# Scratch rows of a two-step Fourier transform laid every other row, so that its DMAs move 48 and 56 rows of one stride

## The chip, the cores and the metric

The kernel runs on one core of one Trainium2 chip. The metric is the device time of one execution in microseconds (us); lower is better. TensorE (PE) multiplies matrices, VectorE (DVE), ScalarE (ACT) and GpSimd (POOL) work on tiles, and SyncE (SP) does nothing here but issue DMAs, one after the other.

## The reference

```python
# x: (8, 3136, 256); w_r, w_i: (256, 256)
X = rfft(x, axis=1)
Yr = Xr @ w_r - Xi @ w_i + b_r
Yi = Xr @ w_i + Xi @ w_r + b_i
Y = soft_threshold(Yr, 0.01) + 1j * soft_threshold(Yi, 0.01)
a = irfft(Y, n=3136, axis=1)
u = a + real(fft(fft(a, axis=1), axis=2))
un = (u - mean(u)) / sqrt(var(u) + 1e-6)          # over the last axis
out = u + relu(un @ w_ch1) @ w_ch2                # 256 -> 1024 -> 256
```

## The kernel before

The sequence of 3136 = 64 x 49 is transformed in two steps, and back in two steps, with a pass through DRAM after each first step, since rows have to change places between partitions and the free axis. There are eight batches `b`. For each of them:

- `p1` multiplies by the 64-point table and folds the inputs `n2` and `49 - n2` into their sum and difference (`fold`). Of the 49 inputs, 24 pairs and one single (number 24 of `NM` = 25) remain. The results go to a DRAM scratch `ad` (for the first batch to four pieces `aq`).
- `p2_f2` (the helper `rows_f2`, line 532) loads the rows that one group of four frequencies `u` needs into a tile `af`: half `i` = 0 at partition 0 and half `i` = 1 at partition 64, one DMA for each half. A half holds 25 rows of sums and 25 rows of differences. Tables `tff` are loaded beside it. Matmuls of line 570 multiply them.
- `p2_w` multiplies by the weights and thresholds; `p2_mix` makes the second Fourier transform's part (scratch `md`, tiles `mq`); `p2_yt` transposes.
- `p2_g2` (line 794) does the first step back: its result is copied by ACT (line 813) into a tile `bev` and stored with two DMAs of line 816 for each `bev` into the DRAM scratch `bd`. A half again is 25 rows of sums and 25 of differences.
- `p3_norm` loads `bd` (tiles `bf`, line 871) and `md` (tiles `mt`, lines 885 to 890), takes the second step back and the norm; `p3_tr`, `p3_mlp1` and `p3_mlp2` transpose and run the two dense layers with their matmuls `h` and `o` (helper `mm3`, line 179). At the end of a group of up to 512 columns, line 982 multiplies `o` by the row scale into a tile `t` on DVE.

Two points matter for what follows. First, `t` shares its two buffers with the copies `bev`:

```python
bev = sb.tile([128, 512], F32, tag="bf" if odd else "bev", bufs=4 if odd else 2, name="bev")   # line 812
t = rb if k else sb.tile([128, 512], F32, tag="bev", bufs=2, name="t")                         # line 981
```

so line 982 can run only when the stores that read an earlier `bev` have landed. Second, every DMA is on SP's one queue, in the order in which the program was laid out, and each takes one of eight semaphores in turn (`DMAHW0` to `DMAHW7`): a DMA is issued only when the one eight places ahead of it has landed.

The order of the work of different batches is written out by due times (each `yield` of a task is one), and a scheduler then orders the instructions. Scratch tensors `ad` and `bd` have the shape `[2, NM, 2, U, D]`: sum or difference, which of 25, half, frequency (32), column (256).

Of the kernel before, what the change touches and what calls it, by code (L numbers as in the profile page):

```python
# [62 lines left out]
def tables():  # L63
    n1 = np.arange(N1)
    n2 = np.arange(N2)

    fwd = np.zeros((2, N1, 2, 2, U))
    inv = np.zeros((2, 2, U, 2, 2, 32))
    n1h = rows_n1()
    for s in range(2):  # L70
        for u in range(U):
            ph = 2 * np.pi * ((n1 * u) % N1) / N1
            if u == 0:
                alt = np.where(n1 % 2, -1.0, 1.0)
                fwd[s, :, s, 0, 0] = 1.0
                fwd[s, :, s, 1, 0] = alt
                inv[s, 0, 0, s] = 1.0
                inv[s, 1, 0, s] = np.where(n1h % 2, -1.0, 1.0)
            else:
                fwd[s, :, s, 0, u] = np.cos(ph)  # L80
                fwd[s, :, s, 1, u] = -np.sin(ph)
                phh = 2 * np.pi * ((n1h * u) % N1) / N1
                inv[s, 0, u, s] = 2 * np.cos(phh)
                inv[s, 1, u, s] = -2 * np.sin(phh)
    tf = np.zeros((2, 64, U, S))
    ti = np.zeros((2, 64, U, 64))
    kp = np.append(np.arange(1, NM), 0)
    P, M = slice(0, NM), slice(NM, 2 * NM)
    for u in range(U):
        t, sg = slot_freqs(u)  # L90
        m = len(t)
        ph = 2 * np.pi * (np.outer(kp, t) % N) / N
        co, si = np.cos(ph), np.sin(ph)
        if u == 0:
            w = np.full(50, 2.0)
            w[[0, 49]] = 1.0
            for c in range(2):
                j = slice(25 * c, 25 * c + 25)
                tf[c, P, 0, j] = co[:, j]
                tf[1 - c, M, 0, j] = -si[:, j]  # L100
                ti[c, j, 0, P] = (co * w)[:, j].T / N
                ti[1 - c, j, 0, M] = (-si * w)[:, j].T / N
        else:
            tf[0, P, u, :m] = co
            tf[0, M, u, :m] = si
            tf[1, P, u, :m] = co * sg
            tf[1, M, u, :m] = -si * sg
            ti[0, :m, u, P] = co.T / N
            ti[0, :m, u, M] = si.T / N
            ti[1, :m, u, P] = (co * sg).T / N  # L110
            ti[1, :m, u, M] = -(si * sg).T / N
    p = np.arange(128)
    ph = 2 * np.pi * (np.outer(p, np.arange(129)) % D) / D
    cs = np.stack([np.cos(ph), np.sin(ph)], 1)
    cs[0, 1, 0] = 1.0
    mask = np.ones((128, 2))
    mask[0] = 0.0
    mask[:, 1] *= -1.0
    first = fwd.reshape(128, 2, 2, 4, 8).transpose(0, 3, 1, 2, 4).reshape(128, 128)
    out = dict(  # L120
        fwd=fwd.reshape(128, 128), fwd0=first, inv=inv.reshape(128, 128),
        tf=tf.reshape(128, U, S), ti=ti.reshape(128, U, 64),
        cs=cs, mask=mask, ident=np.eye(128),
    )
    return {k: np.ascontiguousarray(v, dtype=np.float32) for k, v in out.items()}
# [11 lines left out]
T = 10000  # L137
E = 32
MR = NH + 64 + E

SHAPE0, STEP0 = (0.25, 0.25, 0.6), 0.15
SHAPE, STEP1, STEP = (0.395, 0.569, 0.36), 0.2, 0.25
# [8 lines left out]
def spectral_block(ctx: ExitStack, tc: tile.TileContext, x, w_ri, b_ri, w1, w2,  # L151
# [171 lines left out]

    def pair_rows(t, kp):

        rows = t.shape[2] * t.shape[3] * D
        return bass.AP(t.tensor, t.offset + kp * rows, [[D, 2 * rows // D], [NM * rows, 2], [1, D]])

    def tile_rows(t, i, u, n):

        half = t.shape[3] * D
        return bass.AP(t.tensor, t.offset + i * half + u * D, [[2 * (NM - i) * half + half, 2], [2 * half, NM], [1, n * D]])

    def fold(g, out, copied):

# [11 lines left out]
    def p1_first():  # L347


        aq = [dr.tile([2, NM, 2, 8, D], F32, tag=f"aq{q}", bufs=1, name=f"aq{q}") for q in range(4)]  # L350
        ad1 = dr.tile([2, NM, 2, U, D], F32, tag="ad", bufs=4, name="ad1")
        a_dram[0] = lambda u: (aq[u // 8], u % 8)
        a_dram[1] = lambda u: (ad1, u)

# [11 lines left out]

        def store(q, ev, mb, nn, single):
            if single:
                src = ev[32 * q:32 * q + 16, :D].unsqueeze(1).to_broadcast((16, 2, D))
                return st_eng.dma_start(out=aq[q][:, mb].rearrange("s c u d -> (c u) s d"), in_=src)  # L370
            rows = 16 * D
            src = ev[32 * q:32 * q + 32, :nn * D].rearrange("p (n s d) -> p n s d", s=2, d=D)
            for i in range(2):
                dst = bass.AP(aq[q].tensor, aq[q].offset + (i * NM + mb) * rows, [[D, 32], [2 * rows, nn // 2], [1, D]])
                d = st_eng.dma_start(out=dst, in_=src[:, :, i])
            return d

# [40 lines left out]
        ev, mb = rest[0][:2]  # L418
        for q, c in np.ndindex(4, 2):
            with tc.issue_after(af_ld[3]):  # L420
                st_eng.dma_start(out=ad1[:, mb, c, 8 * q:8 * q + 8].rearrange("s u d -> u s d"),
                                     in_=ev[32 * q + 16 + 8 * c:32 * q + 24 + 8 * c, :D].unsqueeze(1).to_broadcast((8, 2, D)))

    def ask(b, ci, todo, slots, pre):

# [41 lines left out]
    def p1(b):  # L467
# [3 lines left out]
            return  # L471
        for i in (b, b + 1)[:1 + (b % 2 == 0)]:
            if i not in a_dram:
                ad = dr.tile([2, NM, 2, U, D], F32, tag="ad", bufs=4, name=f"ad{i}")
                a_dram[i] = lambda u, ad=ad: (ad, u)
        todo = [(m, 4) for m in range(0, NM - 1, 4)] + [(NM - 1, 1)] * (b % 2 == 0)
        t0, width = T1 if b == 1 else (b - 0.3, 0.75) if b > 2 else (2.0, 0.48)
# [8 lines left out]
        while ci < len(todo):  # L486
            yield T * (t0 + width * ci / len(todo))
            if todo[ci][1] == 1:
                ask(b, ci, todo, slots, pre)
                m, xf = todo[ci][0], pre[ci]  # L490
                g = gtile("g_f1")
                te.matmul(g[:, :D], fwd_f, xf[:, :D], start=True, stop=True)
                ev = xf[:, D:2 * D]
                sc.copy(ev, g[:, :D])
                for r in range(2):
                    st_eng.dma_start(out=a_dram[b + r](0)[0][:, m].rearrange("s c u d -> (c u) s d"),
                                     in_=ev[r * 64:r * 64 + 64].unsqueeze(1).to_broadcast((64, 2, D)))
                ci += 1
                continue
            groups = []  # L500
            for c in range(ci, ci + (1 if b == 1 else 2)):
                ask(b, c, todo, slots, pre)
                i = slots[c][3]
                xf = pre[c - i][:, i * 1024:i * 1024 + 1024]
                groups.append(([gtile("g_f1") for _ in range(2)],
                               [[xf[64 * r:64 * r + 64, p * 512:p * 512 + 512] for p in range(2)] for r in range(2)], xf[0:1, 0:2]))
            quarters(fwd_f, groups)
            for c, (banks, movs, late) in enumerate(groups, ci):
                i, m = slots[c][3], todo[c][0]
                xf = pre[c - i][:, i * 1024:i * 1024 + 1024]  # L510
                for r, g in enumerate(banks):
                    ev = xf[:, r * 512:r * 512 + 512]
                    fold(g, ev, ev[:, D:])
                    st_eng.dma_start(out=pair_rows(a_dram[b](0)[0], m + 2 * r), in_=ev.rearrange("p (s d) -> p s d", d=D))
            ci += len(groups)
# [16 lines left out]
    def rows_f2(b, q, s):  # L532

        u0 = 8 * q
        tag = "tot" if b == 0 and (2 * q + s) % 3 == 2 else "af"
        af = sb.tile([128, 4 * D], F32, tag=tag, bufs=2, name="af")
        ad, u = a_dram[b](u0 + 4 * s)
        load = nc.sync.dma_start
        for i in range(2):
            ld = load(out=af[64 * i:64 * i + 50], in_=tile_rows(ad, i, u, 4))  # L540
        tff = sb.tile([128, 4, S], F32, tag="tff", bufs=3, name="tff")
        load(out=tff, in_=c_tf[:, u0 + 4 * s:u0 + 4 * s + 4, :])
        if b == 0:
            af_ld[2 * q + s] = ld.ins
            done.add(("af", 2 * q + s))
        return af, tff

    def p2_f2(b):


        for q in range(4):
# [12 lines left out]
            for s in range(2):  # L564
                yield base + STEP * F2W * s / 2

                def one(i, t, k, j):
                    rows = slice(64 * i, 64 * i + 50)
                    first = t * D + k * 128 + j * 64
                    return te.matmul(banks[i][64 * j:64 * j + 64, k * 200 + t * S:k * 200 + t * S + S], afs[s][rows, first:first + 64],  # L570
                                     tfs[s][rows, t], start=True, stop=True)
# [221 lines left out]

    def p2_g2(b):

        bd = b_dram[b] = dr.tile([2, NM, 2, U, D], F32, tag="bd", bufs=4, name=f"bd{b}")
        for q in range(4):
            base, STEP, F2W, W0, WW, M0 = clock2(b, q)
            for s in range(2):
# [10 lines left out]
                for i, g in enumerate(banks):  # L810
# [2 lines left out]
                    sc.copy(bev, g)  # L813
                    for h in range(2):
                        j = i ^ h
                        st_eng.dma_start(out=tile_rows(bd, i, 8 * q + 4 * s + 2 * h, 2), in_=bev[64 * j:64 * j + 50])  # L816
        done.add(("b", b))


# [7 lines left out]
    def p3_norm(b):  # L827
# [36 lines left out]
        def load(m, n):  # L864
            mt = sb.tile([128, 4, D], F32, tag="mt", bufs=2, name="mt")
            bfs = [sb.tile([128, 512], F32, tag="bf", bufs=4, name="bf") for _ in range(1 + (n > 1))]
            for r in range(2):
                if n == 1:
                    nc.sync.dma_start(out=bfs[0][64 * r:64 * r + 64, :D], in_=b_dram[b - 1 + r][0, m].rearrange("c u d -> (c u) d"))
                else:  # L870
                    nc.sync.dma_start(out=bfs[r].rearrange("p (s d) -> p s d", d=D), in_=pair_rows(b_dram[b], m + 2 * r))
            for r in (1, 0):
# [213 lines left out]
```

## Time and profile before

| | |
|---|---|
| median of 3 runs | 2291.35 us (2291.03 to 2292.4) |
| profiled execution | 2296.82 us, span of its instructions 2294.9 us |
| PE busy | 1854.8 us, 81% of the span |
| DVE, ACT, POOL busy | 1185.5, 785.8, 537.2 us |
| mean granted clock of TensorE | 0.89 |
| DMA packets' time, of 16 engines | 34.0% of the span on SP's queue |

The profiled execution is 5.5 us above the median, and 1.9 us of it lie outside its span. PE is the busiest engine. The profile's chain of work that ended last follows the execution back from its end, at each step to what released it; a DMA in it is counted from issue to landing.

### The profile page before, as it was taken

The numbers are of one execution on the slowest core, as the hardware profiler recorded it, in microseconds if no ns is written. First come the engines' busy times: TensorE is split into PE (matmuls) and PEld (weight loads), VectorE is DVE, ScalarE is ACT, GpSimd is POOL, SyncE is SP. The second block draws the span as 40 slices with busy tenths as digits, with TensorE's granted clock in tenths as the row PEclk, the third lists the DMA queues.
The fourth block names the chain that finished last, engine by engine and source line by source line (L and its number), as shares of the span: only waits on it lengthen the run. The fifth ranks groups of instructions, "written<-read, shape, count | busy, mean of one in ns | idle before, by whom it ended". The sixth has DMA issues, their size and how long they took to land.

```text
span 2294.9 us, 36930 instructions
## 1 busy us (share of the span) xinstructions
PE 1854.8 (81%) x13447; PEld 1457.6 (64%) x13447; DVE 1185.5 (52%) x2754; ACT 785.8 (34%) x1957; POOL 537.2 (23%) x1005
## 2 busy tenths in 40 slices
PE   6674295887969858988787958989696979898999
PEld 4343174666758647766566747767475758676888
DVE  3553264555646545555454634655463736565554
ACT  1343242333434423433332423323243434342222
POOL 0000132222323212232221412313232323222210
PEclk8776597988989979999898978999898998999999
DMA  5443334334432433324432343322433224224211
GB/s 167 156 132 99 95 117 128 100 99 137 138 108 70 140 116 110 96 68 135 132 117 75 102 141 98 116 83 88 139 125 97 80 86 118 92 59 125 78 33 41
DMA packets 166902, 242.97 MB, mean 106 GB/s; under 512 B 25025, under 2 KB 110657, under 8 KB 166465
## 3 DMA queue, kind: packets, MB, share of 16 engines
q1 hardware_dynamic: 166720, 240.62, 34.0%
q8 instruction: 106, 1.74, 0.3%
q14 instruction: 76, 0.61, 0.1%
HBM read 136.19 MB, written 104.36 MB: 105 GB/s over the span
## 4 chain that ended last, share of the span: by engine, by line
PE 55%; DMA 25%; DVE 8%; SPq 6%; issue 3%; ACT 2%; POOL 1%; DVEq 0%; POOLq 0%; ACTq 0%
PE o L179 21%; PE h L179 17%; DMA bd<-bev 11%; DMA af<-ad 5%; PE g_w L179 5%; DMA af<-aq 2%; PE g_g L808 2%; PE g_f L570 2%; DMA out_dram<-total 2%; PE g_yt L789 2%; SPq L816 1%; SPq L889 1%; PE g_f L439 1%; PE g_ut L932 1%; DVE ut L835 1%
## 5 line engine op out<-in xcount | busy, mean ns | idle before, releaser
L179 PE MATMUL o<-hl,w2h 128*128 128x512 f32 (+2 forms) x832 | 351.5, 423 | 234.8 <-DVE t L982 222.8
L951 DVE SCALAR_TENSOR_TENSOR hl<-h,hh 128x512 fp32r<-128x512 f32 (+2 forms) x416 | 271.6, 655 | 358.2 <-ACT hh L950 344.7
L950 ACT ACTIVATE hh<-h 128x512 fp32r<-128x512 f32 (+2 forms) x416 | 237.6, 572 | 636.7 <-PE h L179 467.2
L179 PEld LDWEIGHTS o<-hl,w2h 128*128 128x128 f32 x832 | 168.7, 203 | 304.7 <-DVE t L982 230.2
L179 PE MATMUL o<-hh,w2l 128*128 128x512 f32 (+2 forms) x832 | 333.7, 401 | 0.0
L179 PE MATMUL o<-hh,w2h 128*128 128x512 f32 (+2 forms) x832 | 333.7, 401 | 0.0
L179 PE MATMUL h<-utl,w1h 128*128 128x512 f32 (+2 forms) x832 | 325.2, 391 | 6.3 <-DVE hl L951 6.3
L179 PE MATMUL h<-uth,w1l 128*128 128x512 f32 (+2 forms) x832 | 320.0, 385 | 0.0
L179 PE MATMUL h<-uth,w1h 128*128 128x512 f32 (+2 forms) x832 | 319.5, 384 | 0.0
L958 POOL TENSOR_TENSOR total<-uth,utl 128x256 f32<-128x256 f32 x200 | 145.0, 749 | 462.9 <-DMA out_dram<-total 306.5
L982 DVE TENSOR_TENSOR t<-o,rb 128x512 f32<-128x512 f32 (+2 forms) x52 | 34.2, 658 | 298.8 <-DMA bd<-bev 259.4
L179 PEld LDWEIGHTS o<-hh,w2l 128*128 128x128 f32 x832 | 168.6, 203 | 31.3
L179 PEld LDWEIGHTS h<-utl,w1h 128*128 128x128 f32 x832 | 160.6, 193 | 40.9 <-DVE hl L951 9.1
L179 PEld LDWEIGHTS o<-hh,w2h 128*128 128x128 f32 x832 | 169.8, 204 | 23.2 <-issue 0.8
L179 PEld LDWEIGHTS h<-uth,w1l 128*128 128x128 f32 x832 | 159.6, 192 | 30.1 <-issue 2.4
L179 PEld LDWEIGHTS h<-uth,w1h 128*128 128x128 f32 x832 | 160.1, 192 | 26.6 <-issue 0.4
L647 DVE SCALAR_TENSOR_TENSOR y<-g_w,small,ks 128x400 f32<-128x400 f32 x128 | 80.2, 627 | 109.9 <-ACT ks L642 55.1
L570 PE MATMUL g_f<-tff,af 50*64 50x50 f32 x4096 | 85.2, 240 | 43.2 <-ACT g_f L458 22.4
L570 PEld LDWEIGHTS g_f<-tff,af 50*64 50x64 f32 x4096 | 76.6, 153 | 65.3 <-ACT g_f L458 25.3
L650 POOL TENSOR_TENSOR Y<-y,m 128x400 f32<-128x400 f32 x56 | 61.6, 1100 | 219.0 <-DVE m L649 206.1
L789 PE MATMUL g_yt<-ident,Y 128*128 128x128 f32 x496 | 89.0, 300 | 27.2 <-POOL Y L650 15.1
L813 ACT COPY bev<-g_g 128x512 f32<-128x512 f32 x128 | 69.2, 588 | 87.7 <-PE g_g L808 56.8
(170 smaller groups left out, 3102.4 us busy)
## 6 DMA issues: line engine op xcount, KB each, us to landing
bd<-bev SPq DMA_DIRECT2D x256, 100.0 KB
bf<-bd SPq DMA_DIRECT2D x96, 256.0 KB
out_dram<-total SPq DMA_DIRECT2D x88, 256.0 KB
af<-ad SPq DMA_DIRECT2D x112, 200.0 KB
ad<-xf SPq DMA_DIRECT2D x84, 256.0 KB
md<-mq SPq DMA_DIRECT2D x112, 192.0 KB
xf<-in_x SPq DMA_DIRECT2D x39, 512.0 KB
mt<-md SPq DMA_DIRECT2D x192, 64.0 KB
```

Of the source, the lines that this page charges most:

```text
L179: last = te.matmul(o, l, r, start=start and i == 0, stop=stop and i == 2)
L439: return te.matmul(banks[i][64 * j:64 * j + 64], mat[rows, rows], movs[i][j], start=True, stop=True)
L570: return te.matmul(banks[i][64 * j:64 * j + 64, k * 200 + t * S:k * 200 + t * S + S], afs[s][rows, first:first + 64], tfs[s][rows, t], sta ...
L647: va.scalar_tensor_tensor(y1, gw, bias[:, c, o:o + 1], ks, op0=ALU.add, op1=ALU.add)
L650: (va if b == 0 or o == 0 else gp).tensor_sub(y[:, o, :, c, :], y1, m)
L789: te.transpose(gt[:, (v * 2 + o) * 128:(v * 2 + o + 1) * 128], z.rearrange("p c w -> p (c w)"), ident)
L808: return te.matmul(banks[i][64 * j:64 * j + 64, cols], tif[rows, 2 * h + v], ys[h][rows, cols], start=True, stop=True)
L813: sc.copy(bev, g)
L950: sc.activation(hh[:, :w], h[:, :w], AF.Relu)
L951: va.scalar_tensor_tensor(hl[:, :w], h[:, :w], 0.0, hh[:, :w].bitcast(F32), op0=ALU.max, op1=ALU.subtract)
L958: gp.tensor_add(total[:, k, cols], uth[:, k, cols].bitcast(F32), utl[:, k, cols].bitcast(F32))
L982: va.tensor_mul(t[:, :w], o, rb[:, :w])
```

## The change

The scratch tensors become `[2 * 56, U, D]`. Even rows belong to half 0 and odd rows to half 1. Of half `i`, rows `i`, `i + 2`, ... hold 24 rows of sums, the single row (row 48 for half 0, row 97 for half 1), and 24 rows of differences. The single is stored once, not as sum and as difference. `tile_rows` now is one run of rows of one stride. `rows_f2` issues three DMAs, not two: 48 rows for each half, and one of two rows (96 and 97, the last of each half) into partitions 48 and 112. `p2_g2` stores 56 rows for each half, of which the last seven lie behind the 49 that are read. The single rows are stored and loaded by two DMAs where there was one. The tables are reordered to match, and the matmuls of line 570 contract over 49 rows, not 50.

```diff
@@ tables: rows of the two halves
-    kp = np.append(np.arange(1, NM), 0)
-    P, M = slice(0, NM), slice(NM, 2 * NM)
+    kp = np.arange(NM)
+    P = [np.append(r, np.arange(NM - 1)) for r in (NM - 1, 2 * NM - 2)]
+    M = [np.arange(NM, 2 * NM - 1), np.arange(NM - 1, 2 * NM - 2)]
@@ constants
+RT = 56
@@ helpers
     def pair_rows(t, kp):
-        rows = t.shape[2] * t.shape[3] * D
-        return bass.AP(t.tensor, t.offset + kp * rows, [[D, 2 * rows // D], [NM * rows, 2], [1, D]])
+        rows = t.shape[1] * D
+        return bass.AP(t.tensor, t.offset + 2 * kp * rows, [[D, 4 * rows // D], [(2 * NM - 1) * rows, 2], [1, D]])
-    def tile_rows(t, i, u, n):
-        half = t.shape[3] * D
-        return bass.AP(t.tensor, t.offset + i * half + u * D, [[2 * (NM - i) * half + half, 2], [2 * half, NM], [1, n * D]])
+    def tile_rows(t, i, u, n, r=RT):
+        rows = t.shape[1] * D
+        return bass.AP(t.tensor, t.offset + i * rows + u * D, [[2 * rows, r], [1, n * D]])
+    def zero_rows(t, c, u=0, n=None):
+        return t[(2 * NM - 2) + (2 * NM - 1) * c, u:u + (n or t.shape[1])]
@@ p1_first, store of the single row (p1 alike)
-                src = ev[32 * q:32 * q + 16, :D].unsqueeze(1).to_broadcast((16, 2, D))
-                return st_eng.dma_start(out=aq[q][:, mb].rearrange("s c u d -> (c u) s d"), in_=src)
+                for c in range(2):
+                    d = st_eng.dma_start(out=zero_rows(aq[q], c), in_=ev[32 * q + 8 * c:32 * q + 8 * c + 8, :D])
+                return d
@@ rows_f2
         for i in range(2):
-            ld = load(out=af[64 * i:64 * i + 50], in_=tile_rows(ad, i, u, 4))
+            load(out=af[64 * i:64 * i + N2 - 1], in_=tile_rows(ad, i, u, 4, N2 - 1))
+        ld = load(out=af[N2 - 1::64], in_=ad[2 * N2 - 2:2 * N2, u:u + 4].rearrange("r u d -> r (u d)"))
@@ p2_f2, one
-                    rows = slice(64 * i, 64 * i + 50)
+                    rows = slice(64 * i, 64 * i + N2)
@@ p2_g2
-        bd = b_dram[b] = dr.tile([2, NM, 2, U, D], F32, tag="bd", bufs=4, name=f"bd{b}")
+        bd = b_dram[b] = dr.tile([2 * RT, U, D], F32, tag="bd", bufs=4, name=f"bd{b}")
-                        st_eng.dma_start(out=tile_rows(bd, i, 8 * q + 4 * s + 2 * h, 2), in_=bev[64 * j:64 * j + 50])
+                        st_eng.dma_start(out=tile_rows(bd, i, 8 * q + 4 * s + 2 * h, 2), in_=bev[64 * j:64 * j + RT])
@@ p3_norm, load of the single row
-                    nc.sync.dma_start(out=bfs[0][64 * r:64 * r + 64, :D], in_=b_dram[b - 1 + r][0, m].rearrange("c u d -> (c u) d"))
+                    for c in range(2):
+                        nc.sync.dma_start(out=bfs[0][64 * r + 32 * c:64 * r + 32 * c + 32, :D], in_=zero_rows(b_dram[b - 1 + r], c))
```

The order of the matmuls on PE and of the work of DVE, ACT and POOL stays the same but for a few neighbours that change places. On SP's queue the program has 1740 DMAs, not 1658. Three places of that queue, with the semaphores that each DMA waits for (the names are tiles and scratch tensors as above, with the numbers of their buffers, and the size is that of the DMA's destination; `PE`, `Activation` and `DVE` are waits for those engines):

The first `af` loads of the program, before:

```order
L316 DMA small_100<-in_b_ri 128x4
L540 DMA af_279<-aq0_114 50x1x1024 x2
L540 DMA af_284<-aq0_114 50x1x1024 x2
L316 DMA ident_98<-c_ident 128x128
L316 DMA csf_330<-c_cs 128x258
```

and after:

```order
L315 DMA small_100<-in_b_ri 128x4
L543 DMA af_280<-aq0_114 48x1024 x2
L544 DMA af_280<-aq0_114 2x1024
L543 DMA af_286<-aq0_114 48x1024 x2
L544 DMA af_286<-aq0_114 2x1024
L315 DMA ident_98<-c_ident 128x128
```

Each tile has one more DMA, and nothing changes places.

Loads of `af` for batch 3 and the first loads of `p3_norm` behind them, before:

```order
L540 DMA af_7792<-ad3_124 50x1x1024 [waits DMAHW3_49,PE_49,Activation_49]
L540 DMA af_7792<-ad3_124 50x1x1024 [waits DMAHW4_49]
L542 DMA tff_7800<-c_tf 128x200 [waits DMAHW5_49]
L540 DMA af_7797<-ad3_124 50x1x1024 [waits DMAHW6_49,PE_49,Activation_49]
L540 DMA af_7797<-ad3_124 50x1x1024 [waits DMAHW7_49]
L542 DMA tff_8582<-c_tf 128x200 [waits DMAHW0_49]
L871 DMA bf_8201<-bd2_126 128x2x256 [waits DMAHW1_49,PE_49,Activation_49]
L871 DMA bf_8202<-bd2_126 128x2x256 [waits DMAHW2_49,PE_49]
L889 DMA mt_8200<-md2_125 32x2x256 [waits DMAHW3_49,DVE_49]
L889 DMA mt_8200<-md2_125 32x2x256 [waits DMAHW4_49]
```

and after:

```order
L543 DMA af_7828<-ad3_124 48x1024 [waits DMAHW7_49,PE_49,Activation_49]
L543 DMA af_7828<-ad3_124 48x1024 [waits DMAHW0_49]
L544 DMA af_7828<-ad3_124 2x1024 [waits DMAHW1_49]
L543 DMA af_7834<-ad3_124 48x1024 [waits DMAHW2_49,PE_49,Activation_49]
L543 DMA af_7834<-ad3_124 48x1024 [waits DMAHW3_49]
L544 DMA af_7834<-ad3_124 2x1024 [waits DMAHW4_49]
L546 DMA tff_7838<-c_tf 128x200 [waits DMAHW5_49]
L546 DMA tff_8621<-c_tf 128x200 [waits DMAHW6_49]
L876 DMA bf_8239<-bd2_126 128x2x256 [waits DMAHW7_49,PE_49,Activation_49]
L876 DMA bf_8240<-bd2_126 128x2x256 [waits DMAHW0_49,PE_49]
L894 DMA mt_8238<-md2_125 32x2x256 [waits DMAHW1_49,DVE_49]
```

Both `af` tiles have a third load, and the first `tff` now stands behind the second `af`. The load of `mt` waited for the semaphore of the first `af` load (`DMAHW3` in both rows of before); now the first `bf` does (`DMAHW7`).

Some ten rows further on, the stores of `bev`, before:

```order
L889 DMA mt_8211<-md2_125 32x2x256 [waits DMAHW6_49]
L816 DMA bd3_128<-bev_7364 2x25x512 [waits DMAHW7_49,Activation_49]
L816 DMA bd3_128<-bev_7364 2x25x512 [waits DMAHW0_49]
L816 DMA bd3_128<-bev_7368 2x25x512 [waits DMAHW1_49,Activation_49]
L816 DMA bd3_128<-bev_7368 2x25x512 [waits DMAHW2_49]
```

and after:

```order
L894 DMA mt_8249<-md2_125 32x2x256 [waits DMAHW4_49]
L820 DMA bd3_128<-bev_7400 56x512 [waits DMAHW5_49,Activation_49]
L820 DMA bd3_128<-bev_7400 56x512 [waits DMAHW6_49]
L820 DMA bd3_128<-bev_7404 56x512 [waits DMAHW7_49,Activation_49]
L820 DMA bd3_128<-bev_7404 56x512 [waits DMAHW0_49]
```

The four stores keep their place; each is 56 rows of 512 elements where it was two groups of 25.

## Rows read from the trace of the kernel before

**Rows 1.** Windows: us, busy us (count) of each engine, clock, DMA share, GB/s.

```profile
0.00:290.00 290.00, 158.56 (x1353) 100.49 (x1354) 115.66 (x275) 84.54 (x218) 16.69 (x43) 0.69 0.41 130
290.00:2110.00 1820.00, 1516.24 (x11201) 1206.96 (x11200) 976.83 (x2278) 653.69 (x1641) 490.36 (x874) 0.91 0.35 107
2110.00:2295.00 185.00, 179.98 (x897) 150.20 (x895) 93.06 (x202) 47.61 (x99) 30.14 (x90) 1.00 0.18 54
```

**Rows 2.** Waits of PE: who, for whom, us in total, times, longest.

```profile
PE o L179 <- DVE t L982: 222.8, 26, 21.9
PE g_g L439 <- ACT ks L642: 48.1, 1, 48.1
...
PE g_yt L789 <- POOL Y L650: 15.1, 3, 7.2
```

**Rows 3.** Waits of DVE, same columns.

```profile
DVE t L982 <- DMA bd<-bev: 259.4, 25, 24.0
```

**Rows 4.** Timeline 664 to 688: start, us, instruction, in brackets idle time and releaser.

```profile
667.93 9.00 SPq L816 DMA_DIRECT2D bd<-bev  x4
...
684.02 0.69 DVE L982 TENSOR_TENSOR t<-o,rb 128x512 f32<-128x512 f32 x1 [15.20 <-DMA bd<-bev]
...
684.77 0.79 PE L179 MATMUL o<-hl,w2h 128*128 128x512 f32 x1 [11.96 <-DVE t L982]
```

**Rows 5.** Timeline 400 to 412, same columns.

```profile
402.21 2.52 SPq L816 DMA_DIRECT2D bd<-bev  x4
...
409.87 0.69 DVE L982 TENSOR_TENSOR t<-o,rb 128x512 f32<-128x512 f32 x1 [5.22 <-DMA bd<-bev]
410.62 0.50 PE L179 MATMUL o<-hl,w2h 128*128 128x512 f32 x1 [1.88 <-DVE t L982]
```

**Rows 6.** Timeline of SP's queue, 770 to 830, same columns.

```profile
790.31 1.40 SPq L540 DMA_DIRECT2D af<-ad  x2
...
794.34 6.66 SPq L871 DMA_DIRECT2D bf<-bd  x2
801.09 3.15 SPq L889 DMA_DIRECT2D mt<-md  x2
...
806.63 4.42 SPq L889 DMA_DIRECT2D mt<-md  x2
...
815.32 2.61 SPq L816 DMA_DIRECT2D bd<-bev  x4
```

**Rows 7.** Chain of the whole run: start, us from issue to landing, what.

```profile
48.36 19.59 DMA af<-aq
...
249.74 11.60 DMA bd<-bev
265.24 3.57 DMA mt<-md
...
793.03 17.45 DMA af<-ad
...
1870.65 2.84 DMA bf<-bd
...
1891.99 7.99 DMA mt<-md
```

**Rows 8.** Chain from 0 to 290 us, shares of that window by line.

```profile
by line: DMA af<-aq 17.9%; DMA bd<-bev 11.4%; SPq L816 6.5%; PE g_w L633 6.4%; DMA af<-ad 4.4%; DMA ad<-xf 3.4%; issue 2.9%; SPq L540 2.8%; PE g_yt L789 2.6%; DMA xf<-in_x 2.5%; PE g_g L808 2.2%; PE g_mix L725 2.1%; PE g_f L570 2.0%; SPq L6
```

**Rows 9.** DMA issues of the page: what, count, KB each.

```profile
bd<-bev SPq DMA_DIRECT2D x256, 100.0 KB
bf<-bd SPq DMA_DIRECT2D x96, 256.0 KB
...
af<-ad SPq DMA_DIRECT2D x112, 200.0 KB
```

**Rows 10.** Windows after one wait, columns as in the first group.

```profile
1107.00:1111.00 4.00, 3.99 (x13) 3.21 (x14) 3.97 (x11) 0.29 (x1) 1.77 (x5) 0.60 0.44 137
1112.00:1178.00 66.00, 66.00 (x490) 52.33 (x489) 41.80 (x103) 29.42 (x74) 22.56 (x38) 1.00 0.40 129
```

More of the change, by code (lines that the diff above doesn't have):

```diff
@@ L98, in tables @@
                 j = slice(25 * c, 25 * c + 25)
[L99 to L102, printed above, removed]
-        else:
[L104 to L111, printed above, removed]
+                tf[c, P[c], 0, j] = co[:, j]
+                tf[1 - c, M[1 - c], 0, j] = -si[1:, j]
+                ti[c, j, 0, P[c]] = (co * w)[:, j] / N
+                ti[1 - c, j, 0, M[1 - c]] = (-si * w)[1:, j] / N
+        else:
+            for c, a in ((0, 1.0), (1, sg)):
+                tf[c, P[c], u, :m] = co * a
+                tf[c, M[c], u, :m] = (si * (a if c == 0 else -a))[1:]
+                ti[c, :m, u, P[c]] = co * a / N
+                ti[c, :m, u, M[c]] = (si * (a if c == 0 else -a))[1:] / N
     p = np.arange(128)
@@ L347, in p1_first @@
     def p1_first():
-        aq = [dr.tile([2, NM, 2, 8, D], F32, tag=f"aq{q}", bufs=1, name=f"aq{q}") for q in range(4)]
-        ad1 = dr.tile([2, NM, 2, U, D], F32, tag="ad", bufs=4, name="ad1")
+        aq = [dr.tile([2 * RT, 8, D], F32, tag=f"aq{q}", bufs=1, name=f"aq{q}") for q in range(4)]
+        ad1 = dr.tile([2 * RT, U, D], F32, tag="ad", bufs=4, name="ad1")
         a_dram[0] = lambda u: (aq[u // 8], u % 8)
@@ L368, in store @@
             if single:
-                src = ev[32 * q:32 * q + 16, :D].unsqueeze(1).to_broadcast((16, 2, D))
-                return st_eng.dma_start(out=aq[q][:, mb].rearrange("s c u d -> (c u) s d"), in_=src)
-            rows = 16 * D
+                for c in range(2):
+                    d = st_eng.dma_start(out=zero_rows(aq[q], c), in_=ev[32 * q + 8 * c:32 * q + 8 * c + 8, :D])
+                return d
+            rows = 8 * D
             src = ev[32 * q:32 * q + 32, :nn * D].rearrange("p (n s d) -> p n s d", s=2, d=D)
             for i in range(2):
-                dst = bass.AP(aq[q].tensor, aq[q].offset + (i * NM + mb) * rows, [[D, 32], [2 * rows, nn // 2], [1, D]])
+                dst = bass.AP(aq[q].tensor, aq[q].offset + ((2 * NM - 1) * i + 2 * mb) * rows, [[D, 32], [4 * rows, nn // 2], [1, D]])
                 d = st_eng.dma_start(out=dst, in_=src[:, :, i])
@@ L420, in p1_first @@
             with tc.issue_after(af_ld[3]):
-                st_eng.dma_start(out=ad1[:, mb, c, 8 * q:8 * q + 8].rearrange("s u d -> u s d"),
-                                     in_=ev[32 * q + 16 + 8 * c:32 * q + 24 + 8 * c, :D].unsqueeze(1).to_broadcast((8, 2, D)))
+                st_eng.dma_start(out=zero_rows(ad1, c, 8 * q, 8), in_=ev[32 * q + 16 + 8 * c:32 * q + 24 + 8 * c, :D])
     def ask(b, ci, todo, slots, pre):
@@ L473, in p1 @@
             if i not in a_dram:
-                ad = dr.tile([2, NM, 2, U, D], F32, tag="ad", bufs=4, name=f"ad{i}")
+                ad = dr.tile([2 * RT, U, D], F32, tag="ad", bufs=4, name=f"ad{i}")
                 a_dram[i] = lambda u, ad=ad: (ad, u)
@@ L495, in p1 @@
                 for r in range(2):
-                    st_eng.dma_start(out=a_dram[b + r](0)[0][:, m].rearrange("s c u d -> (c u) s d"),
-                                     in_=ev[r * 64:r * 64 + 64].unsqueeze(1).to_broadcast((64, 2, D)))
+                    for c in range(2):
+                        st_eng.dma_start(out=zero_rows(a_dram[b + r](0)[0], c), in_=ev[64 * r + 32 * c:64 * r + 32 * c + 32])
                 ci += 1
@@ L868, in load @@
                 if n == 1:
-                    nc.sync.dma_start(out=bfs[0][64 * r:64 * r + 64, :D], in_=b_dram[b - 1 + r][0, m].rearrange("c u d -> (c u) d"))
+                    for c in range(2):
+                        nc.sync.dma_start(out=bfs[0][64 * r + 32 * c:64 * r + 32 * c + 32, :D], in_=zero_rows(b_dram[b - 1 + r], c))
                 else:
```

## The prediction

> **What bounds the kernel now.** I read the windows first, to see in which stretch PE, the busiest engine, has idle time. The reader is to see three stages in [rows 1]. In the first 290 us PE is busy 158.6 us, in the middle 1516.2 of 1820 us, in the last 185 us it hardly idles (180.0 us). So there are 131 us of idle PE at the start, 304 us in the middle, and 5 at the end; only the first two can give anything.
>
> Then the waits of PE say what the idle time is. In the middle one wait makes up most of it: matmul `o` of line 179 waits for `t` on DVE, 222.8 us in 26 waits, the longest 21.9 us [rows 2]. The waits of DVE say what `t` waits for: a landing of `bd<-bev`, 259.4 us in 25 waits [rows 3]. That is the shared buffer: `t` needs a `bev` whose store has landed. At the start the largest single wait of PE is 48.1 us [rows 2], and the chain of that window names its makers: `af<-aq` 17.9%, `bd<-bev` 11.4%, `af<-ad` 4.4%, and SP's own rows at lines 816 and 540 with 6.5% and 2.8% [rows 8].
>
> Then the timeline shows the wait in two forms. In the plain form the stores are issued at once and only their landing is late: issued from 402.21, and `t` goes on at 409.87 after 5.2 us of waiting, of which PE feels 1.9 [rows 5]; or issued from 667.93, and `t` goes on at 684.02, with 12.0 us of idle PE [rows 4]. In the long form the stores are also issued late, because SP stands: four `af` loads are issued from 790.31, and behind them a pair of `bf` takes 6.66 us and two pairs of `mt` take 3.15 and 4.42 us, so that the stores start at 815.32 [rows 6]. The chain shows why: an `af` load issued at 793.03 lands 17.45 us later [rows 7], and SP issues no DMA before the one eight places ahead has landed (the two order pieces of that place, on `DMAHW3`).
>
> Bytes don't explain such landings. A `bf` load of 256 KB lands in 2.84 us; stores of 100 KB take up to 11.60 and loads of 200 KB up to 19.59 [rows 7, 9]. What sets the slow ones apart is their shape: two groups of 25 rows.
>
> By the Trainium skill (DMA: Bandwidth & Descriptors, section "Why a DMA increments its semaphore by 16 and not by 1") a DMA is shared among the largest number of engines, at most 16, that divides the slowest dimension of both sides. That makes 2 engines of 16 for shapes of 50 rows and 2 groups, and 16 and 14 for 48 and 56 rows. The landings in [rows 7] agree with it; no view here names the engines.
>
> **The change part by part.**
>
> *256 stores of `bd`.* A new store moves 112 KB in one run of 56 rows. Its landing isn't in the trace. The nearest rows are loads spread over 128 rows: 2.84 us for 256 KB from below, and from above 7.99 us for a small `mt` load that landed among other traffic [rows 7]. I take 3 us: an undisturbed `mt` load took 3.57 [rows 7], and the traffic that disturbed the other is largely the slow DMAs themselves.
>
> The long waits: some five, of about 20 us (the longest 21.9), about 96 us of the 222.8 [rows 2]. From 794.34 to 815.32 [rows 6], 21 us, SP issues 14 DMAs (two pairs of `bf` and ten of `mt`, of which the order pieces show the first and the last). At 0.65 us each, half of what the undisturbed pair at 790.31 takes, they are 9 us: SP stands for 12. Two further `af` loads stand ahead of the stores and cost 1.4 us, so these are issued 10.6 us sooner. From the issue of the first store to `t` it is 7.7 us in the plain form [rows 5]; two issues and a landing of 3 us make some 3.7, another 4 us. So about 15 us of each go, 75 in all, and some 20 stay.
>
> The other 21 share 127 us, 6 us each. In [rows 5] the stores' issue takes about 2.5 us for four, and the wait of PE, 1.9 us, is smaller than the 3 us or more by which landings fall; in [rows 4] a landing 3 us after issue ends all of 12.0 us. I let 0.5 us of each stay, 10 us. Together 75 + 117, rounded to 190 of the 222.8 us go. If the new landing were 8 us, only the longest waits would shrink, by about 90 us; if 2.8 us, and SP never stood, 215.
>
> *TensorE's clock.* Just after a long wait, from 1107 to 1111, the granted clock is 0.60 of full, that is 2.4 GHz for a fifth of the time and 1.2 GHz for the rest, while PE is busy throughout; with no pause, from 1112 to 1178, it is 1.00 [rows 10]. So PE loses (1 - 0.60) x 4.0 = 1.6 us for one such wait, 42 us for 26. Waits that stay cost it still: I take 35 (bounds 10 and 55, the latter with the pauses of other waits).
>
> *The start.* The 128 loads of `af` shrink to 48 rows and 192 KB, of which the landing again is taken as 3 us. The chain's shares above are 43.0% of 290 us, 125 us [rows 8]. They contain seven slow landings in a row, of 9 to 20 us (as 19.59 and 11.60 in [rows 7]); seven landings of 3 us and 5 us of issue are 26 us in their place. Of the 99 us that are left I take three quarters, 75, since PE has 131 us of idle time there [rows 1] but other work of the chain stands beside it. Bounds: 40 (landing 8 us) and 100.
>
> *The third load of each `af`, and the single rows.* 82 DMAs more on SP's queue at about 0.7 us, 57 us of SP's time. It is hidden where SP waits for other engines; where it isn't, it is in the 1.4 us above. The two-row load is issued 0.7 us behind its sisters and lands beside them. Without cover it would cost all of 57.
>
> By the Trainium skill (DMA: Bandwidth & Descriptors, section "Rules for kernel authors") transfers under 64 KB are mostly overhead and should be joined, which speaks against a third load of 8 KB; its "Anatomy of one DMA" gives about 2 us of fixed cost (for another issue path), so one behind the other the 82 would cost an estimated 164 us. The trace has DMAs in flight side by side, two `bf` in 2.84 us [rows 7], so I count their issue alone.
>
> *Rows that are stored and never read* (12% more bytes), contraction over 49 rows instead of 50 and the new tables cost nothing that counts: they lie inside the landing above, and the matmul's count of columns stays.
>
> *What is late next.* PE's smaller waits don't depend on these DMAs: 15.1 us for `Y` on POOL [rows 2] may come back once more as everything moves together. I give back 15 us.
>
> Sum, against the profiled execution's 2296.8 us: 190 + 35 + 75 - 15 = 285, so 2012 us; the runs shown have a median 5.5 us below that execution, so **2006 us**.
>
> **The rivals.**
>
> *More comes free (1900 us).* The slow DMAs also delay all others that are in flight with them: an `mt` load takes 7.99 us in one place and 3.57 in another [rows 7], and in [rows 6] `bf` and `mt` stand though they are of another shape. If these fall too, PE in the middle would run as at the end, 180 of 185 us [rows 1]: of 304 us idle some 50 stay, the clock gives 55 and the start 100, 409 less; a part of that is optimistic, so 1900.
> By the Trainium skill (same page, same section as first named) a DMA on few engines takes the lowest-numbered ones, so all the 50-row DMAs share the same two, and every DMA on 16 engines has a part behind them. That would make this case; [rows 6] agree, since `bf` and `mt` stand, but show no engine.
>
> *Other waits take the place (2125 us).* SP's queue keeps its order, with 14 DMAs and more ahead of the stores in the long waits. If these keep half their length, the start is held by PE and DVE in turn, and the shorter batches make DVE (977 of 1820 us in the middle, [rows 1]) and POOL late, then 110 + 15 + 45 = 170 go: 2127, less 5.5. The landing at its upper bound of 8 us gives about the same.
>
> *Slower (2335 us).* The landing may be set by rows, not by how they are grouped. Then 56 rows take 12% longer than 50, 12% of the 259.4 us of waits and of the chain's 33 us at the start, 35 us; and two more DMAs for each pair of `af` stand before the stores, 10 to 15 us in all. It decides once a store of 56 rows lands no sooner than one of 50 does. The 2.84 us for 256 KB in 128 rows speak against it [rows 7]. That the change doesn't do what it says falls under this one.
>
> **How the numbers follow.** Forecast 0.62 (its own range 1930 to 2080), more comes free 0.15, other waits 0.17, slower 0.04; 0.02 for a result within 0.2%, about what a measurement of this kernel can tell from no change. The range of 1895 to 2120 us holds the forecast, and the better part of the two neighbours, some 0.8 in all; it takes in the bounds of the landing. Faster by over 0.2%: 0.94; within: 0.02; slower: 0.04.
>
> **What would show it.** After: `af<-ad` and `bd<-bev` in the chain no longer than 5 us; PE's wait for `t` under 50 us in total; SP rows of `bf` and `mt` behind `af` at 1.2 us a pair; the first 290 us shortened by about 75; the middle's clock at 0.95 or above. The prediction is wrong if landings stay above 8 us, or if they fall and PE's idle time turns up at another wait: then the second or the third rival holds.

## The result and the profile after

The changed kernel takes 1921.55 us (median of 4 runs, 1919.39 to 1926.19) against 2291.19 us before: a ratio of 0.839, with a 95% interval of 0.837 to 0.841. The forecast was 2006 us with a range of 1895 to 2120. The direction and the range were right; the saving is 370 us where 285 were forecast.

The windows of the changed kernel, with the same columns as [rows 1], cut where PE has done the same number of matmuls, but for two or three: at its first `h` matmul and at the last stage:

```profile
0.00:198.00 198.00, 151.60 (x1330) 94.38 (x1331) 114.75 (x273) 82.31 (x214) 14.97 (x41) 0.77 0.65 189
198.00:1733.00 1535.00, 1471.22 (x11226) 1181.09 (x11225) 986.32 (x2280) 658.86 (x1646) 495.12 (x879) 0.98 0.44 129
1733.00:1918.00 185.00, 179.53 (x895) 149.76 (x893) 92.91 (x201) 47.36 (x98) 29.80 (x88) 1.00 0.19 54
```

and of the kernel before, cut at the same places:

```profile
0.00:285.50 285.50, 154.06 (x1330) 96.56 (x1331) 114.64 (x273) 82.51 (x214) 15.96 (x41) 0.69 0.41 130
285.50:2110.00 1824.50, 1520.74 (x11223) 1210.88 (x11223) 977.85 (x2279) 655.72 (x1646) 491.09 (x875) 0.91 0.35 107
```

The start is 87.5 us shorter, the middle 289.5 us, and the end the same 185 us. Of the middle's 289.5 us, PE's busy time gives 49.5 us, with the same matmuls: the granted clock is 0.98 where it was 0.91. The other 240 us are idle time of PE, which falls from 303.8 to 63.8 us.

PE's waits in the whole of the changed kernel (columns as in [rows 2]):

```profile
PE o L178 <- DVE t L987: 29.6, 9, 6.3
PE o L178 <- DVE hl L956: 14.6, 12, 5.4
...
PE g_g L442 <- ACT ks L646: 7.2, 1, 7.2
...
PE g_yt L793 <- POOL Y L654: 3.1, 2, 2.2
```

and what `t` waits for on DVE:

```profile
DVE t L987 <- DMA bd<-bev: 53.6, 21, 8.5
```

The wait for `t` is 29.6 us where it was 222.8, and the single wait of 48.1 us at the start is 7.2 [rows 2]. On DVE 259.4 us [rows 3] became 53.6 us, in 21 waits where there were 25: the waits are nearly all still there, but 2.6 us long on average instead of 10.4, and 12 of the 21 no longer reach PE.

SP's queue at the place that answers to [rows 6]:

```profile
615.95 0.83 SPq L543 DMA_DIRECT2D af<-ad  x2
616.84 0.55 SPq L544 DMA_DIRECT2D af<-ad  x1
617.50 0.79 SPq L543 DMA_DIRECT2D af<-ad  x2
618.34 0.51 SPq L544 DMA_DIRECT2D af<-ad  x1
618.96 2.43 SPq L546 DMA_DIRECT2D tff<-c_tf  x2
621.91 1.17 SPq L876 DMA_DIRECT2D bf<-bd  x2
623.17 1.29 SPq L894 DMA_DIRECT2D mt<-md  x2
...
630.59 1.83 SPq L820 DMA_DIRECT2D bd<-bev  x4
```

From the first `af` load to the first store it is 14.6 us; before it was 25.0 [rows 6], although two DMAs more stand between. A pair of `mt` takes 1.29 us. SP still stands a little, in the pair of `tff` (2.43 us). The chain's longest DMAs are now:

```profile
617.86 6.63 DMA af<-ad
654.99 5.25 DMA bd<-bev
...
1078.13 5.83 DMA af<-ad
1084.02 5.73 DMA bf<-bd
1118.05 5.32 DMA bd<-bev
```

where single landings of up to 19.59 us stood [rows 7]; the share of all DMAs in the chain fell from 25% to 5% of the span.

### The profile page after: what moved, and what is told of

The parts are those of the page before. It is cut to its first block, busy times and chain, and to the rows that moved or that the text cites. A ratio compares the mean times of both kernels' runs of the same rounds, so it can differ in the third digit from the quotient of the medians.

```text
span 1917.6 us, 37007 instructions
## 1 busy us (share of the span) xinstructions
PE 1802.4 (94%) x13447; PEld 1425.2 (74%) x13447; DVE 1194.0 (62%) x2754; ACT 788.5 (41%) x1957; POOL 539.9 (28%) x1005
## 4 chain that ended last, share of the span: by engine, by line
PE 75%; DVE 8%; DMA 5%; SPq 3%; ACT 2%; issue 2%; POOL 1%; DVEq 0%; ACTq 0%; POOLq 0%
PE o L178 26%; PE h L178 25%; PE g_w L178 9%; PE g_g L812 3%; PE g_f L574 2%; PE g_yt L793 2%; DMA bd<-bev 2%; PE g_ut L937 2%; PE g_g L442 2%; PE g_f L442 1%; DMA af<-ad 1%; PE g_mix L732 1%; SPq L894 1%; DVE ut L839 1%; PE g_w L637 1%
## 5 line engine op out<-in xcount | busy, mean ns | idle before, releaser
L178 PE MATMUL o<-hl,w2h 128*128 128x512 f32 (+2 forms) x832 | 335.2, 403 | 44.7 <-DVE t L987 29.6
L178 PE MATMUL h<-utl,w1h 128*128 128x512 f32 (+2 forms) x832 | 321.3, 386 | 4.0 <-DVE hl L956 4.0
L178 PE MATMUL o<-hh,w2l 128*128 128x512 f32 (+2 forms) x832 | 322.4, 388 | 0.0
L178 PE MATMUL o<-hh,w2h 128*128 128x512 f32 (+2 forms) x832 | 321.3, 386 | 0.0
L178 PEld LDWEIGHTS o<-hl,w2h 128*128 128x128 f32 x832 | 160.8, 193 | 105.1 <-DVE hl L956 37.5
L178 PEld LDWEIGHTS o<-hh,w2l 128*128 128x128 f32 x832 | 160.6, 193 | 28.5
L178 PEld LDWEIGHTS o<-hh,w2h 128*128 128x128 f32 x832 | 161.2, 194 | 21.8 <-issue 0.8
L574 PEld LDWEIGHTS g_f<-tff,af 49*64 49x64 f32 x4096 | 74.1, 149 | 29.4 <-issue 10.1
L574 PE MATMUL g_f<-tff,af 49*64 49x50 f32 x4096 | 82.2, 235 | 8.0 <-ACT g_f L461 2.5
L171 POOL TENSOR_TENSOR Xl<-xx,Xh 128x400 fp32r<-128x400 f32 x54 | 55.6, 1044 | 108.8 <-ACT Xh L604 108.5
```

Of the source, the lines that this page charges most:

```text
L171: gp.tensor_sub(out_, full, hi.bitcast(F32))
L178: last = te.matmul(o, l, r, start=start and i == 0, stop=stop and i == 2)
```

## The experiments

Nine kernels were run. The theory (A) was that a DMA of 50 rows in two groups uses two of the 16 DMA engines and keeps them busy for long, and that all that is issued with it waits. The rivals were (B) that one run of one stride, or the layout in DRAM, matters and not the number of engines, and (C) that the buffer that `t` shares with `bev` is the whole matter. Each kernel was timed beside the kernel before, on the same chip; ratios are to that. The diffs show the lines that issue the DMAs; tables and the other accesses of the same scratch were changed to match.

**One part alone: the stores.** Scratch `bd` as in the change, `ad` and its loads as before:

```diff
-        bd = b_dram[b] = dr.tile([2, NM, 2, U, D], F32, tag="bd", bufs=4, name=f"bd{b}")
+        bd = b_dram[b] = dr.tile([2 * RT, U, D], F32, tag="bd", bufs=4, name=f"bd{b}")
-                        st_eng.dma_start(out=tile_rows(bd, i, 8 * q + 4 * s + 2 * h, 2), in_=bev[64 * j:64 * j + 50])
+                        st_eng.dma_start(out=tile_rows_n(bd, i, 8 * q + 4 * s + 2 * h, 2), in_=bev[64 * j:64 * j + RT])
```

> The new rows for bd alone (stores of 56 rows, tables and single rows to match); ad and aq and the loads of af as in the kernel before. Theory A (a DMA of 50 rows in two groups of 25 keeps two DMA engines busy for long, and everything issued with it queues behind): the plain waits of t go, the long ones behind four af loads stay by half or more; PE's wait for t falls from 222.8 to 60 to 100 us, the time to about 2100 us (2060 to 2150). Theory B (it is the run of one stride, or the layout in DRAM, not the number of engines): about the same here. Theory C (the buffer that t shares with bev is the whole matter): nearly the full gain, below 1980.

Measured: 2089.23 us, ratio 0.913 (0.908 to 0.918).

```profile
PE o L184 <- DVE t L1002: 122.5, 14, 18.6
```

The time is as theory A had it (B expected the same), and not as C had it. Fewer waits reach PE, 14 where there were 26. The four long ones behind `af` loads stay, at 16.0 to 18.6 us. Of the plain form not all went: five waits of 8 to 10 us are left, so the sum of 122.5 us is above the 60 to 100 expected. Two of these five, at 600 and 1100 us, are in the chain, where a store of 56 rows still takes 11.5 and 11.4 us to land.

**One part alone: the loads.** Scratch `ad` and `aq` as in the change, `bd` and its stores as before:

```diff
-            ld = load(out=af[64 * i:64 * i + 50], in_=tile_rows(ad, i, u, 4))
+            load(out=af[64 * i:64 * i + N2 - 1], in_=tile_rows(ad, i, u, 4, N2 - 1))
+        ld = load(out=af[N2 - 1::64], in_=ad[2 * N2 - 2:2 * N2, u:u + 4].rearrange("r u d -> r (u d)"))
```

> The new rows for ad and aq alone (loads of 48, 48 and 2 rows, tables to match); bd and the stores of bev as in the kernel before, two groups of 25. Theory A: the long waits of t shrink to the plain form, the plain ones of 4 to 8 us stay; PE's wait for t falls from 222.8 to 100 to 140 us, the start gets shorter by some 50 us; time about 2130 us (2080 to 2180). The savings of this and of the stores alone add up to about the whole 370 us or somewhat less. Theory C: little gain, 2230 or above, since the stores still land late.

Measured: 2049.22 us, ratio 0.896 (0.887 to 0.905).

```profile
PE o L182 <- DVE t L1000: 108.6, 23, 14.0
```

Nearly as many waits as before, none longer than 14.0 us. That is the form expected, but the saving of 237 us is more than was expected, and more than that of the stores (197 us). The start is 66 us shorter (the first `h` matmul stands at 218.8 us, before at 285.2), where 50 were expected. The two savings add up to 434 us, where the whole change's 370 or somewhat less were expected: part of the lost time goes away whichever of the two is mended. That the two kinds of DMA slow each other on the same engines would explain it, but wasn't shown by itself.

**The same layout, other numbers of rows.** The first changes two rows:

```diff
-RT = 56
+RT = 58
```

> The changed kernel with stores of 58 rows in place of 56, all else the same: one run of one stride, 3.6% more bytes, layout unchanged but for two rows at its end. Theory A, by the rule of the Trainium skill (DMA: Bandwidth & Descriptors, section on why a DMA increments its semaphore by 16 and not by 1): 58 = 2 x 29 goes to 2 engines again, so stores land in 6 us and more and the time is that of the new loads alone, about 2130 us (2080 to 2190). Theory B: 1920 to 1935 us, as the run is still of one stride.

Measured: 2099.43 us, ratio 0.918 (0.910 to 0.926). The order of PE's and DVE's instructions is the same as in the changed kernel. Two rows more, with one stride as before, cost some 180 us; theory B is out. The time isn't quite that of the new loads alone, which theory A named: it is 50 us more, with stores of 116 KB where those have 100 KB. The second takes three rows away:

```diff
-                        st_eng.dma_start(out=tile_rows(bd, i, 8 * q + 4 * s + 2 * h, 2), in_=bev[64 * j:64 * j + RT])
+                        st_eng.dma_start(out=tile_rows(bd, i, 8 * q + 4 * s + 2 * h, 2, 53), in_=bev[64 * j:64 * j + 53])
```

> The changed kernel with stores of 53 rows: three rows and 5% of the bytes less than 56, the same stride, layout and nearly the same order. Theory A, by the rule of the Trainium skill (DMA: Bandwidth & Descriptors, section on why a DMA increments its semaphore by 16 and not by 1): 53 is a prime, so one engine moves all of it. A store then keeps that engine busy for about twice the time that 58 rows took on two, so slower than the 2099 us of 58 rows: 2250 us or more (2180 to 2500). A rival by which rows or bytes set the landing: 1915 to 1922 us.

Measured: 2356.4 us, ratio 1.031 (1.027 to 1.034), slower than the kernel before although its loads are the new ones. PE's wait for `t` with 58 and with 53 rows:

```profile
PE o L178 <- DVE t L987: 129.6, 23, 13.2
```

```profile
PE o L178 <- DVE t L987: 233.6, 23, 19.2
```

and the longest stores in the chain, first of 58 rows, then of 53:

```profile
156.32 12.66 DMA bd<-bev
178.06 11.11 DMA bd<-bev
...
366.95 10.67 DMA bd<-bev
```

```profile
222.62 17.67 DMA bd<-bev
448.32 18.04 DMA bd<-bev
628.66 17.96 DMA bd<-bev
```

In the chain 56 rows land in 5.3 us at worst, 58 in 12.7, 53 in 18.0. Neither rows nor bytes nor stride order them so; the largest divisor up to 16 does: 14, 2 and 1. By the Trainium skill (DMA: Bandwidth & Descriptors, section "Why a DMA increments its semaphore by 16 and not by 1") that divisor is the number of engines; these three times agree with it, though no view names an engine.

The trace says more than its views. It records each update that the DMAs make to the semaphore of a landing, and from their times the updates of each store can be counted, and its landing told from the last of them. All 256 stores of a kernel have the same count:

| rows of a store | largest divisor up to 16 (of two groups, 2) | updates of its semaphore | us to landing, middle one of 256 |
|---|---|---|---|
| 2 x 25 (kernel before) | 2 | 3 | 9.2 |
| 2 x 25 (new loads) | 2 | 3 | 7.4 |
| 56 | 14 | 15 | 2.5 |
| 58 | 2 | 3 | 8.7 |
| 53 | 1 | 2 | 13.0 |
| 64 | 16 | 16 | 2.4 |

The count is one more than the divisor, and 16 at 16. So a store is divided among as many as the divisor says, in the kernel before too, and the landings follow it; what makes the one update more isn't shown.

**The kernel before, with a buffer of its own for `t`.**

```diff
-t = rb if k else sb.tile([128, 512], F32, tag="bev", bufs=2, name="t")
+t = rb if k else sb.tile([128, 512], F32, tag="tt", bufs=1, name="t")
```

> The kernel before, with t in a buffer of its own and not in one of the two of bev; every DMA as before. Theory C (the shared buffer is the cause): PE's wait for t nearly vanishes and the time falls below 2050 us. Theory A: the wait for t goes, but the next copies into bev wait for the same stores, bf loads land as late and af loads hold the queue as before, so waits of PE turn up elsewhere: 2120 to 2230 us.

Measured: 2086.96 us, ratio 0.912 (0.907 to 0.918), with the DMAs as slow as they were: the middle one of the stores still lands in 9.2 us. So this edit is worth some 200 us, more than theory A gave it, and it isn't the whole matter, against C. Waits of PE in this kernel:

```profile
PE o L179 <- DVE hl L951: 80.2, 20, 15.2
PE g_g L439 <- ACT ks L642: 47.2, 1, 47.2
```

and the wait of the copies into `bev`, in the kernel before and in this one:

```profile
ACT bev L813 <- DMA bd<-bev: 23.7, 6, 6.5
ACT bev L813 <- DMA bd<-bev: 67.4, 15, 12.4
```

As theory A had it, the copies into `bev` wait longer for the stores, and matmul `o` waits 80.2 us for `hl`, where it was 11.7 us before. But most of the 80.2 us doesn't stand behind these copies. Four waits of 13.3 to 15.2 us, 56 us in all, go back through POOL to a store of `out_dram`, a DMA of 256 KB whose shape no kernel here changes; one of them:

```profile
1221.44 1.62 SPq L986 DMA_DIRECT2D out_dram<-total  x2
...
1235.84 2.22 POOL L958 TENSOR_TENSOR total<-uth,utl 128x256 f32<-128x256 f32 x4 [27.54 <-DMA out_dram<-total]
...
1241.18 0.58 PE L179 MATMUL o<-hl,w2h 128*128 128x256 f32 x1 [14.27 <-DVE hl L951]
```

The start's wait of 47.2 us is untouched. The scheduler gave this kernel another order: counted place by place, a third of PE's matmuls stand elsewhere, and parts of SP's queue too. How much of the 200 us is the buffer's own and how much the order's wasn't separated.

**The changed kernel, with the same buffer.** The same edit on the changed kernel:

> The changed kernel with t in a buffer of its own. What is left of the wait for t is 29.6 us of PE's idle time in 9 waits. If nothing takes its place, and the clock's dips go with it: 25 to 45 us less, 1880 to 1900 us. If the next copies into bev wait in its place: 0 to 10 us less.

Measured: 1860.3 us (5 runs, 1854.8 to 1860.8), ratio 0.813 (0.811 to 0.815). The wait for `t` is gone from PE's list, and nothing as large took its place:

```profile
PE o L178 <- DVE hl L956: 15.5, 11, 3.5
PE g_yt L793 <- POOL yz L663: 7.7, 2, 4.8
```

61 us less are more than the 25 to 45 expected. The wait itself was 29.6 us; the page shows PE busy 1777.1 us where the changed kernel has 1802.4, another 25 us at a higher clock (0.972 for 0.958). Here too a third of PE's matmuls stand elsewhere, and how much of the gain is the new order's was not separated.

**Stores of 64 rows** (`RT = 64`, the whole half of `bev`):

> The changed kernel with stores of 64 rows (128 KB), by the rule on 16 engines in place of 14, 14% more bytes; each engine moves 4 rows in both. Theory A: no difference beyond 0.5%, since an engine's share is the same 8 KB; the order of the program moves a little in places.

Measured: 1912.07 us, ratio 0.836 (0.834 to 0.838), an interval that overlaps that of the changed kernel. 14% more bytes cost nothing that shows; as expected, a division among 14 or 16, four rows each, is alike.

**One load of 49 rows** for each half of `af`, without the third load:

> The changed kernel with one load of 49 rows for each half of af in place of 48 and a third load of two rows. By the rule 49 rows go to 7 engines of 16, 28 KB each in place of 12. It tells the price of the third load against that of fewer engines. Theory A: slower by 10 to 60 us, since four loads then keep 7 engines busy more than twice as long; if the third loads' issue is what counts, faster by 5 to 20 us.

Measured: 1930.45 us, ratio 0.8455 (0.843 to 0.848), some 15 us slower than the changed kernel by the ratios (9 us between the medians, which weren't taken side by side). PE's wait for `t` is 35.1 us for 29.6. Each of these loads has 8 updates of its semaphore, one more than 7, the largest divisor of 49 up to 16, and the middle one of them lands in 5.5 us, for some 4.5 with 48 rows. So the third load is worth its issue, but by little.

**Both mends together**, a buffer for `t` and 64 rows:

> The changed kernel with both: t in a buffer of its own, stores of 64 rows. Apart, they took 61 us and 9 us off the changed kernel's 1921.55 us. If the two have causes of their own: about 1851 us (1845 to 1858). If the 64 rows helped only by letting t go sooner, nothing is left for them once t has its own buffer: 1855 to 1865 us, the same as the buffer alone.

Measured: 1857.47 us (5 runs, 1855.54 to 1862.4), ratio 0.812 (0.810 to 0.813): no different from the buffer alone by the intervals, though the median lies in both ranges that were named, so it doesn't tell the two cases apart. It is as fast as any kernel here, 64 us or 3% faster than the changed one, and nearly all of it comes with the edit of `t`, in the order that goes with it.

## Why the prediction was right, and where its sizes were off

*What bounds the kernel* was right: the late stores behind `t`, and the start. The wait for `t` lost 193 us; 190 were forecast. The long form went as described: the stores follow the first `af` load by 14.6 us where they followed by 25.0. Where four waits of 19.5 to 21.9 us stood, four of 4.4 to 6.3 us are left; the forecast let some 4 us of each of five stay.

*The landing of 3 us* fits the stores, of which the middle one lands in 2.5 us. For the loads of `af` it was too low: the middle one takes some 4.5 us. In the chain a store of 5.3 us and an `af` load of 6.6 us stay; the condition that none there be longer than 5 us was missed by a little.

*The start* gave 87.5 us for 75. PE's idle time there fell from 131 to 46 us. Three quarters of the 99 us of slow chain was too careful; nearly nine tenths went.

*TensorE's clock* gave 49.5 us in the middle for 35. The forecast kept part of the loss for waits that stay, and more than half of those that stay on DVE don't stop PE at all. That this is the whole of the difference isn't shown.

*What is late next* is the step that failed: "PE's smaller waits don't depend on these DMAs", with 15 us given back. Other idle time in the middle fell instead, from 81.0 to 34.2 us (303.8 less 222.8, 63.8 less 29.6), 47 us, so this term is 62 us off. The smaller waits did depend on these DMAs, as the chain of the kernel before shows for PE's wait for `Y` on POOL:

```profile
963.07 15.51 DMA out_dram<-total
...
978.74 2.76 POOL total L958 x4
981.50 0.98 POOL Y L650
...
985.39 0.90 PE g_yt L789 x3
```

SP issues four `af` loads from 957.86 and two stores of `out_dram` right behind them. The second lands 15.51 us later. POOL waits for it before it makes `total`, and `Y` comes after `total`, so that PE stands for 7.0 us at `g_yt`. The second such wait, of 7.2 us, has the same form, and a third wait of PE, of 8.9 us, goes back through ACT to a slow `af` load itself:

```profile
443.95 10.79 DMA af<-ad
1509.55 14.99 DMA out_dram<-total
```

These three came to 23 us, and all the others in the middle were of 4 us or less. In the changed kernel no store of `out_dram` takes more than 5.4 us to land, though its shape is the same, and PE's wait for `Y` is 3.1 us where it was 15.1 [rows 2].

The errors are 3 us for `t`, 12.5 for the start, 14.5 for the clock and 62 for the smaller waits, 92 us in all, which is what lies between the forecast 285 us and the 377 us between the two profiled executions.

*The rivals.* The result lies nearest to "more comes free" (1900 us), and so do its parts: idle time in the middle fell by 240 us (254 there), the middle's busy time by 49.5 (55), the start by 87.5 (100). Its mechanism, DMAs of another shape that are late with the slow ones, is seen in [rows 6], gone from the same place now, and it is what the wait for `Y` shows. So the forecast was right in what bounds the kernel, and the result lies 85 us under it by a mechanism that it named but gave a chance of 0.15; the range holds the result because it took in a part of that rival. "Other waits take the place" was wrong in the changed kernel; its own sum gives 2121 us, not 2125. "Slower" was wrong for 56 rows and is what 53 rows do, for a reason that the rival didn't name.

*Readings.* Two were a little off, and neither moves the forecast much: half of the pair's 1.40 us [rows 6] is 0.70 us for one issue, not 0.65, and the chain of the kernel before has landings of stores up to 15.63 us, not only the 11.60 shown.

*Extra rows and loads.* Bytes that are stored and never read cost nothing that shows, at 56 and at 64 rows. The third load costs less than one load of 49 rows does. By the Trainium skill (DMA: Bandwidth & Descriptors, section "Rules for kernel authors") transfers under 64 KB should be joined; here the split into a large and a small one is the faster form, by 9 to 15 us, since the joined load has 49 rows and not 48.

## What to carry to other kernels

Before the bytes of a DMA, look at the count of its slowest dimension on both sides: 56 rows here took 1922 us, 58 took 2099 and 53 took 2356. Rows that nobody reads are cheap if they give that count a large divisor up to 16. When slow DMAs go, DMAs of other shapes that were in flight with them land sooner too, and so do waits shrink that seemed to have nothing to do with them; follow each wait back to the landing before you call it independent. And a buffer shared between a store's source and a product of another stage can turn a late store into idle time of the busiest engine; here a buffer of its own, with the order that came with it, gave 3% more at no cost in DMAs.

## What the runs showed of the hardware

A DMA on few engines delays others that use many. Before, a store of `out_dram` of 256 KB took 15.51 us to land behind four slow `af` loads; in the changed kernel none takes more than 5.4. With stores of 53 rows, the ones with 2 updates of their semaphore, a `tif` load of 128 KB behind four such stores takes 13 to 15 us in the chain of that kernel, while the middle one of these loads takes 2.7 us there:

```profile
98.23 13.12 DMA tif<-c_ti
...
127.60 14.68 DMA tif<-c_ti
```

And a single DMA's shape can cost more than all its bytes: three rows fewer (106 KB for 112) made the kernel 435 us slower.
